# Loading a unit's imaginary gates ahead of its real ones, an earlier range check and a new hand-written order in a gated linear attention and soft-MoE kernel

## The chip, the cores and the metric

The kernel runs on 1 core of a Trainium2 chip. Its time is in device microseconds (us). Three runs of the kernel before gave 259.94, 262.14 and 263.29 us, so the median is 262.14 us; a separate execution was profiled.

## The reference

Inputs are q, k, v, a_re, a_im (each 4 x 8 x 768 x 48, float32) and the weights phi, w1, w2 of a soft mixture of experts. First a gated linear attention with complex gates, one step per token:

```python
mag = sqrt(a_re**2 + a_im**2); scale = minimum(mag, 0.999) / (mag + 1e-6)
ar, ai = a_re * scale, a_im * scale
for t in range(S):
    new_re = ar[t] * S_re - ai[t] * S_im
    new_im = ar[t] * S_im + ai[t] * S_re
    S_re, S_im = new_re + outer(k[t], v[t]), new_im
    y[t] = q[t] @ S_re
```

The result, 3072 tokens of 384 channels, goes through the mixture: `logits = x @ phi`; a softmax over the tokens gives 32 slot inputs; each of 8 experts computes `relu(slot @ w1) @ w2` (384 to 1024 to 384) for its 4 slots; a softmax over the slots mixes them back.

## The kernel before, in words

The attention is done in blocks of 128 tokens in polar form. A *unit* holds blocks of up to four batches; there are seven units, 0 and 6 of half size, since batches 2 and 3 lag one unit behind. Of a unit u the steps are, by their names in the order:

- `la{u}` (`load_a`, lines 620 to 626) loads the real gates `ar` and, as its second step, the imaginary gates `ai`, three DMAs of 256 KB each (two of 192 KB in unit 6). Both live in a pool with one buffer per name, so a load must wait until the unit before has read its own. Unit 0 is loaded by `load_first` and counts as two gate groups, `g0` and `g1`, so that unit u is group `g{u+1}`.
- `g` (`gates`, line 683): Ln of `ar` on ACT (line 689), Exp (691), a product into `ai` (DVE 695), a square (ACT 702 or DVE 700), Ln (704), a DVE step (706), Exp (708), a last DVE step (710). `t` (line 715): arctan of `ai` on ACT.
- `p{u}.{j}` (`phase`, 747): prefix sums of `ai` on PE (`sums`, 745, led by a carry matmul on tile `tk`, 743), a rounding (ACT 757 or DVE 755), a DVE step (760). `e{u}.{j}` (`logs`, 784): the same sums of `ar`, then two Exps on ACT (805, 807). `w` (`wave`): an absolute value (DVE 776) and two sines. `k` (`carry`): small steps that end in a PE transpose (734) and a copy to `tk`.
- `h{u}.{j}` (`mults`, 816): three products of q and k with these factors, each on DVE (814) or POOL (812). `M{u}` (`mixed`, 828): four DMAs on SP's queue that copy pieces into the tile `hm`, two after the second product, two after the third.
- `c` (`score`, 862, PE 867, then masked on DVE 879, or on ACT 881 and POOL 882), `a` (`attend`, PE 917 and 923, the result copied to `yT`), `x`, `D`, `f` (transposes, state, tokens) per batch; `l`, `s`, `sh`, `me`, `si` of the mixture's softmax; `hd`, `tn`, `ex`, `ou`, `er`, `mi` its experts, and outputs (`mi`: PE 296, a copy, a store).
- `q`, `v` load q and k, and v; `w_x` loads 1 MB of w1 or w2, in four pieces of 256 KB for x below 12. `T` and `L` preload the ACT table sets for sines and for logarithms. `zz` are pairs of matmuls with no use but activity on PE. `gd` (`ranges`, 1083) is a range check in six steps; its fifth is a PE matmul (1101).

All of this is sequenced by the string `ORDER` (line 306): each word runs a task's next step, and a star sends an operation that ACT or DVE could do (or DVE or POOL) to the other engine. `_InOrder` pins every engine, SP's DMA queue too, to this order. A DMA of a task named `la`, `q`, `v` or `w_` also waits for the last PE instruction traced before it, and a DMA on SP waits until it and those ahead of it under way come to at most 1.3 MB:

```python
for s, name in reversed(self.sent):
    n += s
    if n > UNDER_WAY:
        self.after(ins, name)
        break
```

PSUM serves most results through four buffers named `tr`.

Of the kernel before, what the change touches and what calls it, by code (L numbers as in the profile page):

```python
# [303 lines left out]


ORDER = """
    L0 g0 g0 g0 q1.1 g0* g1 g1 g1 g0 g1 g1 g0 g1 g0 g1 g0 g1 T0 t0 e0.2 e0.0 e0.1 e0.0 e0.1 t1 e0.2 L1 e0.0 e0.2 k0 la1 p0.1 e0.2
    e0.0 e0.1 p0.2 p0.0 p0.0 h0.0* p0.2* g2 g2 p0.1* p0.2 w0.2 p0.0 h0.2 la1 w_1 e0.1 T1 w0.2 w0.2 p0.1 w0.0 k0 q1.0 w_2 w0.0 w0.0
    zz10 g2* g2* h0.2 k0 h0.2 zz5 h0.1 zz13 zz6 h0.0 h0.1 h0.0 k0* M0 t2 p1.2 L2 g2 p1.2 g2 g2 M0 p1.2 v1 zz9 h0.1 p1.1 g2 w1.2
    p1.0 p1.1 p1.0 zz0 p1.1 T2 w1.2 q1.2 c0.0 e1.2 e1.2 w1.2 e1.1 L3 e1.2 p1.0 e1.2 c0.0* e1.0 la2 e1.1 e1.1 x0.0 w1.0 h1.2 e1.1  # L310
    h1.1 e1.0* e1.0 e1.0 la2 a0.0 h1.2 h1.0 x0.1 M1 a0.0 c0.1 x0.0* h1.2* q2.0 x0.0 x0.1 g3 g3 x0.1* T3 w1.0 w1.0 f0.0 c0.1* M1
    w_4 zz14 g3* a0.1 zz3 f0.0 zz12 w_0 q2.2 a0.1* zz1 zz4 k1 g3 h1.0 k1 D0.1 t3 k1* f0.1 D0.0 h1.1 h1.0 p2.2 h1.1 L4 g3 f0.1
    D0.0* D0.1 c0.2 p2.1 g3 q2.1 p2.2 c0.2 p2.0 g3 p2.2 p2.1* c0.3 w2.2 g3 a0.2 T4 w2.2 w2.2 c0.3 p2.0* e2.2 p2.1 a0.2* e2.2 e2.1
    p2.0 e2.1 e2.0 w2.0 L5 e2.2 e2.2 la3 e2.0 a0.3 e2.1 h2.2 x0.2 e2.1 h2.2 e2.0 x0.2 e2.0 la3 x0.2 c1.0 h2.1 k2 f0.2 D0.2 a0.3
    c1.0* D0.2 f0.3 f0.3 f0.2* x0.3 l0 x0.3* k2 c1.1 l0 h2.2* M2 g4 g4 l0 x0.3* h2.0 T5 w2.0 a1.0 g4* w2.0 D0.3 h2.1* k2 a1.0 l0*
    g4 c1.1* x1.0 D0.3 x1.0* h2.0 h2.0 M2 h2.1* x1.0 f1.0 a1.1 D1.0 f1.0* t4 v2 D1.0 a1.1 x1.1 x1.1* p3.2 p3.2* p3.2 x1.1 l0 q3.0
    w3.2 q3.2 p3.0 L6 g4 D1.1 s0 p3.0 g4 c1.2 c1.2 v3 q3.1 p3.1 g4 p3.0 c1.3 T6 w3.2 a1.2 p3.1* w3.2 g4 D1.1 p3.1 e3.2 e3.2 L7
    e3.2 s0 e3.0 c1.3* e3.1 e3.2 la4 a1.2 e3.1* w3.0 e3.0 la4 x1.3 h3.2 e3.0 a1.3 x1.3* e3.0 x1.3* e3.1 e3.1 h3.2 f1.1 h3.0 a1.3
    x2.0 f1.1* k3 x2.0 x1.2 x2.0 x1.2* c2.0 x1.2* g5 g5 T7 w3.0 w3.0 c2.0* D1.2 k3 D1.2 h3.2* h3.1 g5* f1.2 c2.1 k3 s0 a2.0 l1
    f1.2 M3 D2.0 a2.0* f1.3 l1 s0* c2.1* s0 M3 g5 t5 D1.3 w_3 h3.0* a2.1 s0 D1.3 h3.1* f1.3 D2.0 L8 g5 h3.0 f2.0 l1 f2.0* a2.1 l1*  # L320
    x2.1 p4.2 g5 q4.0 q4.2 p4.0 x2.1 g5 h3.1 l1 q4.1 x2.1 s1 p4.2 g5 p4.0 p4.1 c2.2 p4.2 e4.0 p4.0 c2.2 e4.0* e4.0 p4.1* e4.1 e4.2
    e4.0 p4.1 e4.1 e4.1 w4.2 s1 e4.2 la5 e4.1 e4.2 c2.3 e4.2 h4.2* w4.0 x2.2 c2.3* T8 w4.2 x2.2* x2.2* D2.1 a2.2 w4.0 D2.1 h4.0
    h4.1 a2.2 w4.2 la5 x2.3 x2.3 h4.2 w4.0 a2.3 x2.3* a2.3 x3.1 k4 x3.1* D2.2 h4.0* D2.2 x3.1* L9 g6 g6 M4 c3.0 l2 f2.2 f2.3 s1
    l2* c3.0* h4.2 M4 g6* f2.2* h4.1 a3.0 s1* f2.3* k4 l2 a3.0 l2 k4* x3.0 x3.0* c3.1 g6 x3.0 c3.1* h4.0* D2.3 D2.3 D3.0 l2 q5.2
    h4.1 s1 g6 a3.1 T9 t6 s1 g6 D3.0 v4 L10 g6 c3.2 c3.2* g6 p5.0 p5.1 a3.1 D3.1 p5.0 p5.1 q5.1 c3.3 p5.1 q5.0 s2 v5 p5.0 D3.1
    w5.0 s2 e5.2 c3.3 e5.2* x3.2 e5.1 e5.1 e5.2 e5.2 p5.2 x3.2 e5.0 h5.2 e5.1 p5.2* e5.1 e5.0 e5.0 a3.2 h5.1* x3.2 la6 e5.0 la6
    p5.2 T10 w5.0 f2.1 a3.2* x3.3 a3.3 w5.2 c4.0 w5.2 h5.0 f2.1 w5.2 x3.3 x3.3 w5.0 h5.2 a3.3* L11 g7 k5 g7 D3.2 x4.1 s2 s2* D3.2
    h5.2* c4.0* x4.1 x4.1* h5.1 l3 M5 l3* M5 a4.0 c4.1 x4.0 g7* f3.3 a4.0 x4.0 q6.2 h5.0 l3 x4.0 c4.1* D3.3 l3* a4.1 g7* g7 v6 w_5
    f3.3 k5 D3.3 f3.0 a4.1 k5* f3.0* h5.1 f3.1 f3.2 D4.0 h5.0 D4.1 f3.1* g7 c4.2 D4.0 q6.1 T11 t7 f3.2 p6.1 L12 g7 p6.1 c4.2* w_6
    p6.2 p6.0 p6.0 D4.1 g7 p6.0 p6.1 c4.3 e6.2 p6.2 e6.1 q6.0 p6.2 c4.3 e6.1 e6.2 e6.0 w6.2 e6.2 e6.0 e6.2 l3 T12 w6.2 we w_8 w6.2  # L330
    a4.2 h6.2 a4.2* L13 e6.0 w6.0 s3 e6.1 s2 s2 h6.2 h6.2 e6.0 w_7 M6 e6.1 a4.3 c5.0 M6 a4.3 c5.0* f4.2 x4.2 f4.2 T13 w6.0 x4.2*
    s3 w_9 l4 w6.0 h6.1 h6.1 h6.0* h6.0 a5.0 l4* c5.1 x4.2 l4 w_10 h6.0 s3 h6.1* a5.0 l4* s3 x4.3 D4.2 c5.1 x4.3 f4.0 c5.2 D4.2 l4
    f4.0* L14 s4 x4.3 s4 wf w_11 a5.1 a5.1 c5.2 zz8 s4 D4.3 D4.3 s3 s4* w_14 c5.3 a5.2 w_13 w_15 a5.2 f4.3 f4.3* s3 f5.0 f4.1 f5.1
    f5.1* w_16 f4.1* c5.3* a5.3 f5.0 a5.3 s4 l5 zz2 l5* s4 l5 w_17 l5* l5 me s5 f5.3 me sh f5.3* me w_12 me f5.2 s5 me s5 me me
    f5.2* s5 me s5 s5 zz11 sh ze si si zz15 sh hd sh er4 hd w_22 hd er2 hd hd hd w_21 hd gd er0 er4 hd hd w_18 hd tn0 er3 er4 tn0
    er3 er2 tn0* tn0 er1 er3 er2 ex0 hd w_19 gd ex0 ex1 er4 w_20 hd ex0 tn1 er1 tn1 tn1* er3 er0 ex0 tn1* er5 er0 er1 ex1 ex0 ex1
    ex0 ex1 er2 ex0 w_23 ex1 ex0 ou0 er1 ex1 ex1 er0 ou0 mi0.0 mi0.1 mi0.3 mi0.0* er5 mi0.4 ex2 er5 mi0.1* mi0.3* ex1 mi0.0 ou1
    mi0.4 er5 mi0.1 mi0.3 mi0.4 ex2 ex2 ou1 mi0.5 mi1.2 mi0.2 mi1.4 ex2 mi0.5 mi0.5 mi1.2* mi1.2 mi1.1 ex2 mi1.3 mi1.4* mi0.2
# [873 lines left out]
```

## Time and profile before

| | us |
|---|---|
| median of three runs | 262.14 |
| lowest, highest | 259.94, 263.29 |
| profiled execution | 262.23 |
| its span, first to last instruction | 260.7 |
| PE, DVE, ACT, POOL busy | 223.1, 189.5, 187.3, 62.3 |

The span leaves out 1.5 us around the first and the last instruction. An engine's busy time is not its bound: a wait counts only where it moves the chain of work to the end. In the views, a number in brackets is the idle time of the engine ahead of an instruction, with what ended it; `PEclk` is the granted TensorE clock as a share of 2.4 GHz.

### The profile page before, as it was taken

What the parts mean: (1) busy time and instruction counts of PE and PEld (TensorE: products, weight loads), DVE (VectorE), ACT (ScalarE), POOL (GpSimd) and SP (SyncE); (2) the same over time, 40 slices, a digit from 0 to 9 for tenths busy, and PEclk for the clock granted to TensorE, in tenths of its full rate; (3) what the DMA queues carried; (4) which work ended last, traced back from release to release, by engine and by line L of the source; (5) the groups of instructions that cost most, each with busy time, mean ns of one, the idle gap of its engine ahead of it and who ended that gap; (6) DMA issues with size and microseconds to landing.
All of it is one profiled execution on the core that took longest, in us unless ns stands there. A gap on an engine that the chain in (4) does not pass through costs nothing.

```text
span 260.7 us, 10985 instructions
## 1 busy us (share of the span) xinstructions
PE 223.1 (86%) x4828; PEld 177.1 (68%) x4828; DVE 189.5 (73%) x342; ACT 187.3 (72%) x296; POOL 62.3 (24%) x81
## 2 busy tenths in 40 slices
...
GB/s 168 277 265 259 285 158 247 256 250 190 275 127 157 283 173 282 42 270 185 198 109 64 166 263 146 162 125 231 252 254 240 240 291 425 424 400 343 370 363 137
DMA packets 28630, 60.96 MB, mean 234 GB/s; under 512 B 3232, under 2 KB 7584, under 8 KB 27040
## 3 DMA queue, kind: packets, MB, share of 16 engines
...
HBM read 49.17 MB, written 4.72 MB: 207 GB/s over the span
## 4 chain that ended last, share of the span: by engine, by line
PE 67%; DMA 12%; DVE 9%; ACT 5%; issue 3%; SPq 1%; DVEq 0%
PE qd L867 12%; PE qd L917 7%; PE qd L923 7%; PE lp L745 6%; PE up L745 5%; PE tp L852 4%; PE hp L230 4%; PE op L260 4%; DMA wx<-in_w_dram 4%; PE db L896 3%; DMA hm<-qe 3%; DMA ar<-in_aa_dram 3%; PE xp L931 2%; PE lg L115 2%; DVE scT L879 2%
## 5 line engine op out<-in xcount | busy, mean ns | idle before, releaser
L745 PE MATMUL lp<-cst,ar 128*128 128x128 f32 x144 | 20.9, 290 | 9.5 <-DVE ar L710 9.5
L879 DVE TENSOR_TENSOR scT<-qd,cst 128x1024 f32<-128x1024 f32 x16 | 19.5, 1221 | 11.9 <-ACT yT L106 7.4
L745 PEld LDWEIGHTS lp<-cst,ar 128*128 128x128 f32 x144 | 20.0, 203 | 10.5 <-DVE ar L710 10.0
L917 PE MATMUL qd<-scT,vt 128*48 128x128 f32 x352 | 23.8, 277 | 2.0 <-DVE scT L879 1.7
L745 PEld LDWEIGHTS up<-cst,ai 128*128 128x128 f32 x144 | 21.2, 213 | 4.4 <-ACT ai L715 1.7
L745 PE MATMUL up<-cst,ai 128*128 128x128 f32 x144 | 21.9, 297 | 2.6 <-ACT ai L715 1.4
L867 PE MATMUL qd<-e 32*128 32x128 f32 x384 | 23.0, 294 | 0.2 <-DVE scT L879 0.2
L106 ACT COPY yT<-qd 128x512 f32<-128x512 f32 x18 | 10.6, 592 | 16.9 <-PE qd L923 9.7
L917 PEld LDWEIGHTS qd<-scT,vt 128*48 128x48 f32 x352 | 18.2, 122 | 6.4 <-DVE scT L879 2.7
L867 PE MATMUL qd<-q 32*128 32x128 f32 x416 | 21.5, 274 | 0.0
L596 ACT ACT_TABLE_LOAD x15 | 19.2, 1283 | 1.3 <-PEq L1195 1.0
L867 PEld LDWEIGHTS qd<-e 32*128 32x128 f32 x384 | 16.3, 185 | 4.6 <-issue 1.9
L882 POOL TENSOR_SCALAR_AFFINE_SELECT scT<-scT 128x1024 f32<-128x1024 f32 x8 | 8.8, 1102 | 43.3 <-ACT scT L881 43.3
L867 PE MATMUL qd<-hm 32*128 32x128 f32 x352 | 18.3, 270 | 0.0
L599 ACT ACT_TABLE_LOAD x14 | 18.0, 1283 | 0.2
L867 PEld LDWEIGHTS qd<-q 32*128 32x128 f32 x416 | 17.2, 187 | 0.8 <-ACT d L106 0.6
L896 PE MATMUL db<-vt,kt 128*32 128x48 f32 x960 | 14.3, 208 | 3.4 <-issue 1.9
L896 PEld LDWEIGHTS db<-vt,kt 128*32 128x32 f32 x960 | 11.9, 110 | 6.6 <-issue 3.6
L762 POOL COPY cr<-fc 128x4 f32<-128x4 f32 x15 | 3.7, 250 | 51.0 <-DVE fc L760 50.8
L814 DVE TENSOR_TENSOR q<-q,fc 128x1024 f32<-128x1024 f32 (+1 forms) x13 | 14.6, 1140 | 0.2
L867 PEld LDWEIGHTS qd<-hm 32*128 32x128 f32 x352 | 14.6, 187 | 0.0
L812 POOL TENSOR_TENSOR qe<-qe,fc 128x512 f32<-128x512 f32 x8 | 11.9, 1506 | 9.7 <-DMA ar<-in_aa_dram 5.1
...
## 6 DMA issues: line engine op xcount, KB each, us to landing
...
```

Of the source, the lines that this page charges most:

```text
L106: self.nc.scalar.copy(out=out, in_=in_)
L230: self.nc.tensor.matmul(out=hp[x][32 * g : 32 * g + 32, :], lhsT=zs[hi][:, c, g, :], rhs=w1_chunk(12 * hi + 4 * c + g)[:, x * 512 : (x + 1 ...
L596: ACT.preload_act_table_set(LNEXP)
L599: ACT.preload_act_table_set(TRIG)
L745: PE.matmul(out=out[:, b], lhsT=gate[:, b, P * j : P * j + P], rhs=tri, start=not u, stop=not u or b == b1 - 1)
L812: POOL.tensor_tensor(out=out[:, w], in0=in0[:, w], in1=in1[:, w], op=ALU.mult)
L814: DVE.tensor_tensor(out=out, in0=in0, in1=in1, op=ALU.mult)
L867: PE.matmul(out=qd[:, i, P * g : P * g + P], lhsT=feat(u, g, c, 1, b)[r], rhs=feat(u, g, c, 0, b)[r], start=c == 0, stop=c == 2,)
L879: DVE.tensor_tensor(out=t, in0=sc, in1=mask.unsqueeze(1).unsqueeze(1).broadcast_to([P, 4, 2, P]), op=ALU.mult)
L896: PE.matmul(out=db[o, 3 * g + c], lhsT=kt[u, b][:, g, c, o], rhs=vt[u][:, b - _span(u)[0], 4 * g + i], start=True, stop=True)
L917: PE.matmul(out=o(g, i), lhsT=vt[u][:, b - _span(u)[0], 4 * g + i], rhs=scT[u, b][:, i, g], start=True, stop=not s)
L923: PE.matmul(out=o(g, i), lhsT=st[s - 1, b][r, 3 * g + c], rhs=feat(u, g, c, 0, b)[r], start=False, stop=c == 2)
```

## The change

`load_a` keeps its order (`ar`, then `ai`) in unit 1. From unit 2 on its first step takes the buffer of `ai` and loads it, and its second step does so for `ar`; each buffer is now asked for at the step that loads it.

```diff
     def load_a(u):
-        ar[u] = io.tile([P, UB, HD], F32, name="ar")
-        ai[u] = io.tile([P, UB, HD], F32, name="ai")
         b0, b1 = _span(u)
-        load(ar[u][:, b0:b1], aa[u, 0][:, b0:b1])
-        yield "la1"
-        load(ai[u][:, b0:b1], aa[u, 1][:, b0:b1])
+        parts = [(ar, "ar", 0), (ai, "ai", 1)]
+        if u == 1:
+            for held, name, _ in parts:
+                held[u] = io.tile([P, UB, HD], F32, name=name)
+        for held, name, k in parts if u == 1 else parts[::-1]:
+            if k != (u > 1):
+                yield "la1"
+            if u > 1:
+                held[u] = io.tile([P, UB, HD], F32, name=name)
+            load(held[u][:, b0:b1], aa[u, k][:, b0:b1])
```

`ORDER` is new throughout. It has the same words but two (`T13` and `L14` are gone, two of 29 table preloads); 91 steps change their engine by a star. Its beginning, up to the third unit, and its end, from the mixture's `ou2` on:

```diff
-    L0 g0 g0 g0 q1.1 g0* g1 g1 g1 g0 g1 g1 g0 g1 g0 g1 g0 g1 T0 t0 e0.2 e0.0 e0.1 e0.0 e0.1 t1 e0.2 L1 e0.0 e0.2 k0 la1 p0.1 e0.2
-    e0.0 e0.1 p0.2 p0.0 p0.0 h0.0* p0.2* g2 g2 p0.1* p0.2 w0.2 p0.0 h0.2 la1 w_1 e0.1 T1 w0.2 w0.2 p0.1 w0.0 k0 q1.0 w_2 w0.0 w0.0
-    zz10 g2* g2* h0.2 k0 h0.2 zz5 h0.1 zz13 zz6 h0.0 h0.1 h0.0 k0* M0 t2 p1.2 L2 g2 p1.2 g2 g2 M0 p1.2 v1 zz9 h0.1 p1.1 g2 w1.2
-    p1.0 p1.1 p1.0 zz0 p1.1 T2 w1.2 q1.2 c0.0 e1.2 e1.2 w1.2 e1.1 L3 e1.2 p1.0 e1.2 c0.0* e1.0 la2 e1.1 e1.1 x0.0 w1.0 h1.2 e1.1
-    h1.1 e1.0* e1.0 e1.0 la2 a0.0 h1.2 h1.0 x0.1 M1 a0.0 c0.1 x0.0* h1.2* q2.0 x0.0 x0.1 g3 g3 x0.1* T3 w1.0 w1.0 f0.0 c0.1* M1
-    w_4 zz14 g3* a0.1 zz3 f0.0 zz12 w_0 q2.2 a0.1* zz1 zz4 k1 g3 h1.0 k1 D0.1 t3 k1* f0.1 D0.0 h1.1 h1.0 p2.2 h1.1 L4 g3 f0.1
+    L0 g0 g0 g1 g0 g0* g1 g1 g0 g1 g1 g0 g1 g0 g1 T0 t1 g0 t0 g1 e0.2 k0 e0.0 e0.1 la1 e0.2 L1 e0.2 e0.0 e0.2 p0.2 p0.1 p0.2* e0.0
+    e0.0 h0.0 p0.2 p0.0 la1 e0.1 w_1 e0.1 e0.1 g2 p0.0* g2 w0.2 T1 w0.2 p0.1* p0.1 q1.0 p0.0 k0 h0.1 w0.0 k0 h0.2 g2* w0.0 g2* zz4
+    zz13 zz14 w0.0 q1.1 w0.2 h0.2 k0 zz1 h0.2 M0 t2 M0 w_2 h0.0 q1.2 L2 g2 h0.1 h0.0 p1.2 h0.1 g2 p1.1 p1.0 p1.2 g2 la2 c0.0 p1.2
+    p1.0 p1.1* w1.2 T2 w1.2 w1.2 g2 p1.1 zz9 e1.2 p1.0 e1.1 e1.0 e1.2 L3 e1.2 c0.0* w1.0 e1.1 e1.2 h1.2 la2 e1.1 h1.2 e1.0* e1.1
+    h1.1 a0.0 zz10 M1 x0.0 a0.0 e1.0 e1.0 x0.1 x0.0 h1.0 x0.0 g3 v1 w_0 c0.1 zz5 zz0 h1.2* M1 x0.1* x0.1* w_4 q2.1 q2.0 g3 c0.1*
+    T3 w1.0 q2.2 w1.0 a0.1 g3* g3 f0.0 zz12 a0.1* k1 zz3 zz6 f0.0 h1.0 h1.1 k1 h1.0 k1* D0.1 D0.0 f0.1 t3 L4 g3 h1.1 p2.2 D0.0
...
-    mi1.5 mi0.2 mi1.1* mi1.3* mi1.5* mi1.1 mi1.4 ex2 ex2 ex2 mi1.3 mi1.0 mi1.5 ou2 ou2 mi1.0* bh mi2.2 mi1.0 mi2.1 mi2.4 mi2.3
-    mi2.2* mi2.2 mi2.4* mi2.5 mi2.4 mi2.3 mi2.1* zz7 gd mi2.3 mi2.5* gd mi2.1 mi2.5 gd mi2.0 gd mi2.0* mi2.0
+    ex2 mi1.3 mi1.1* mi1.2* ex2 mi1.5* mi1.3* mi1.0 mi1.4 ex2 zz2 mi1.2 ou2 ou2 bh mi2.3 mi2.5 mi2.3 mi2.1 mi2.5* mi2.1 mi2.2
+    mi0.2 mi1.1 mi1.5 mi1.3 zz7 mi2.0 mi2.3 mi2.2* mi2.5 mi2.0 mi2.0 mi2.1 mi2.2 mi2.4 mi2.4 mi2.4
```

Elsewhere the range check's six steps stand ahead of `ou0`, the first of them before the last batches' attention; `w_3`, which came after `M3`, now comes after `la3` and ahead of `M2`; `v3` comes after `M3` where it came before `la4`; `la4`'s and `la6`'s first steps (now `ai`) come behind their units' last `p` instead of their last `e` or later.

## Rows read from the trace of the kernel before

**Rows 1.** Busy time by stretch (start:end, length, then busy us and count by engine).
```profile
9.50:24.00 14.50, 7.77 (x34) 5.30 (x34) 9.09 (x28) 12.10 (x22) 1.45 (x2) 1.00 0.78 259
24.00:31.00 7.00, 5.64 (x23) 4.78 (x24) 6.36 (x9) 5.63 (x5) 0.44 (x1) 0.52 0.84 269
42.00:54.00 12.00, 6.79 (x141) 4.42 (x141) 9.68 (x14) 10.71 (x11) 3.27 (x6) 1.00 0.84 245
60.00:214.00 154.00, 148.67 (x3786) 125.34 (x3782) 119.04 (x185) 122.62 (x195) 53.16 (x63) 1.00 0.63 196
219.80:250.00 30.20, 29.81 (x525) 18.50 (x524) 17.44 (x51) 10.04 (x20) 0.00 (x0) 1.00 0.97 386
```
**Rows 2.** Timeline of ACT at 43 us.
```profile
43.17 1.48 ACT L689 ACTIVATE ar<-ar 128x1536 f32<-128x1536 f32 x1 [2.57 <-issue]
```
**Rows 3.** Line 689, 36 to 48 us, and tile ar, 36 to 46: unit 2's loads.
```profile
L689 ACTq EVENT_SEMAPHORE  x1: 3084/3084/3084, 39.7 to 39.7; - x1
...
DMA to landing us min/median/max: 2.5/2.9/4.7
```
**Rows 4.** Tile ar, 62 to 69 us: the same for unit 3.
```profile
DMA to landing us min/median/max: 2.4/2.8/3.2
```
**Rows 5.** Timeline of SP's DMA queue, 36 to 75 us.
```profile
37.21 1.28 SPq L618 DMA_DIRECT2D ar<-in_aa_dram  x3
38.60 2.21 SPq L618 DMA_DIRECT2D ai<-in_aa_dram  x3
42.87 2.13 SPq L839 DMA_DIRECT2D hm<-qe  x2
48.62 8.00 SPq L618 DMA_DIRECT2D wx<-in_w_dram  x8
68.15 5.05 SPq L839 DMA_DIRECT2D hm<-qe  x4
```
**Rows 6.** Timeline of DVE, 16 to 24 us.
```profile
16.84 0.68 DVE L814 TENSOR_TENSOR qe<-qe 128x512 f32<-128x512 f32 x1
17.96 0.42 DVE L776 TENSOR_SCALAR fc<-fc 128x512 int32<-128x512 int32 x1
20.03 1.96 DVE L695 TENSOR_TENSOR ai<-ai,gt 128x384 f32<-128x384 f32 x4 [0.92 <-ACT gt L691]
```
**Rows 7.** Timeline of DVE, 38 to 42 us: the products of unit 1.
```profile
39.75 1.22 DVE L814 TENSOR_TENSOR qe<-qe,fc 128x1024 f32<-128x1024 f32 x1
```
**Rows 8.** Chain of waits in order of time: a copy into hm, and score c1.2.
```profile
47.47 3.98 DMA hm<-qe
...
84.44 1.55 PE qd L867 x48
```
**Rows 9.** Timeline of PE, 49 to 56 us.
```profile
52.67 0.39 PE L743 MATMUL up<-sf,tk 128*128 128x512 bf16 x1 [2.02 <-ACT tk L106]
54.43 0.40 PE L867 MATMUL qd<-hm 32*128 32x128 f32 x8
```
**Rows 10.** Groups of instructions of the whole run.
```profile
L695 DVE TENSOR_TENSOR ai<-ai,gt 128x384 f32<-128x384 f32 x22 | 10.8, 550 | 3.0 <-ACT gt L691 3.0
...
L596 ACT ACT_TABLE_LOAD x15 | 19.2, 1283 | 1.3 <-PEq L1195 1.0
```
**Rows 11.** Waits of PE, 60 to 214 us.
```profile
PE db L896 <- issue: 1.9, 1, 1.9
```
**Rows 12.** Timeline of all engines, 241 to 255 us.
```profile
241.95 1.33 SPq L303 DMA_DIRECT2D out_dram<-vt  x3
...
253.57 0.19 PE L1101 MATMUL gp<-cst,good 128*1 128x1 f32 x2 [1.40 <-DVE good L1098]
```
**Rows 13.** Stretches of the end: last two numbers are DMA share and GB/s.
```profile
242.00:244.00 2.00, 2.00 (x63) 1.76 (x65) 2.00 (x4) 1.06 (x2) 0.00 (x0) 1.00 0.97 394
254.00:256.00 2.00, 0.19 (x1) 0.00 (x0) 0.12 (x1) 0.59 (x1) 0.00 (x0) 1.00 0.96 353
256.00:258.00 2.00, 0.00 (x0) 0.00 (x0) 0.00 (x0) 0.00 (x0) 0.00 (x0) 0.52 0.33 108
```

More of the change, by code (lines that the diff above doesn't have):

```diff
@@ L315 @@
[L315 to L338, printed above, removed]
@@ new lines @@
+    D0.1 p2.2 g3 c0.2 p2.1 c0.2 p2.0 g3 c0.3 p2.2 la3 p2.0 p2.1* w2.2 g3 p2.1 f0.1* a0.2 e2.2 p2.0 c0.3* e2.1 T4 w2.2 w2.2 e2.0
+    la3 e2.2 L5 e2.2 e2.2 a0.2* e2.1 c1.0 w2.0 e2.1 e2.0 h2.2 e2.1 x0.2 e2.0 e2.0 a0.3 x0.2 x0.2 a0.3 h2.1 w_3 h2.2 f0.2 f0.2* k2
+    c1.0* M2 D0.2 D0.2* l0 h2.0 x0.3 f0.3 l0 f0.3 x0.3* g4 a1.0 x0.3* g4 T5 w2.0 a1.0* w2.0 h2.2* D0.3 c1.1 l0 D0.3* l0* M2 g4*
+    x1.0 k2 h2.0* f1.0 c1.1* x1.0* v2 q3.2 g4 a1.1 x1.0* k2 h2.1 x1.1 t4 f1.0* h2.1 p3.2 x1.1* h2.0* x1.1* p3.0 p3.1 a1.1 p3.2* L6
```

24 lines of the change are left out of this document (22 added, 2 removed).

## The prediction

> **What bounds the kernel now.** I read four views in this order. First the busy time by stretch, cut where PE changes its manner: the reader is to compare PE's busy time with the length of each stretch. From 60 to 214 us PE is busy 148.67 of 154.00 us and from 219.80 to 250 us 29.81 of 30.20, so there PE is the bound; its holes lie at the start, 6.73 us (14.50 - 7.77) from 9.5 to 24 us and 5.21 us (12.00 - 6.79) from 42 to 54 us [rows 1]. Second the waits of PE in the long middle: of its 5.3 us of holes the longest, 1.9, is "issue", in which no other engine is to blame [rows 11]. An order can win little there. Third the timelines of ACT, DVE and SP around the hole at 42 to 54 us. Fourth the end, where the reader is to look at the DMA columns: from 242 to 256 us they are 0.97 busy in the first stretch and 0.96 in the last, at 394 and 353 GB/s, and 0.33 after that [rows 13]. The last 15 us are shared by PE and the stores.
>
> Gains can therefore come from three places: the two early holes, and the end.
>
> **The change part by part.** The base is the profiled execution's 262.23 us (1.5 us of it outside the span); it lies 0.09 us above the median of 262.14, which I take off at the end.
>
> *ai ahead of ar.* In unit 2 ACT stood idle 2.57 us until 43.17 us ahead of Ln [rows 2], and its queue's semaphore wait of 3084 ns from 39.7 us names the DMA of ar: the three pieces took 2.5, 2.9 and 4.7 us to land [rows 3]. They were issued from 37.21 us and ai's right behind them, at 38.60 [rows 5]. In unit 3 the third piece took 3.2 us, with ai issued behind it too [rows 4]. With ai gone ahead (its last reader on PE, the sums of `p`, comes before those of `e`) ar should land like that: 4.7 - 3.2 = 1.5 us sooner. The bounds are 0 and the whole idle time of 2.57. In units 1 and 3 to 6 I cost the edit at nothing: the first consumer of ai is the product on line 695, and all its idle time, 3.0 us, is put down to ACT, none to a load [rows 10]; the cover is the two ACT passes ahead of it, and without them ai would cost its landing time. An early ai also stands in SP's queue and holds what is behind it until PE has passed the last sum of ai; in units 3 to 6 that is only ar and the copies of M, which wait for later work anyway.
>
> *The new order around unit 1.* Between the carry k0 and the product of g2, DVE gets three operations ahead: h0.1's first product and h0.2's, 0.68 each, and an absolute value, 0.42, together 1.78 us; at that place DVE was idle 0.92 [rows 6]. (What comes to DVE before k0, a product of 0.68 from POOL and a rounding of about 0.4 from ACT, is what went out.) So g2, its arctan, unit 1's sums and with them the last e of unit 1 come 1.78 - 0.92 = 0.86, say 0.9 us later, and so does the issue of ar. Bounds: 0, if ar of unit 1 lands sooner since q1.1 no longer goes ahead of it, and 1.8. What is left of the gain at the sums p2.2, which began at 52.67 after a wait of 2.02 us for ACT [rows 9], is 1.5 - 0.9 = 0.6.
>
> *SP's queue at the same place.* The next PE step but one, c0.2, reads hm from 54.43 us [rows 9]; the last copy into hm was issued at 47.47 and landed at 51.45 (47.47 + 3.98) [rows 8], which leaves 2.98 us. In the new order v1 (three pieces) and w_0 (four) go between M1's two halves, and q2.0 (two) goes behind: five pieces more. Held to 1.3 MB under way, pieces went at 8.00 / 8 = 1.00 us each [rows 5], which makes 5.0 us. Against it M1's first half can leave when its second product is done, at 40.97 (39.75 + 1.22) [rows 7], where it left at 42.87 behind ai [rows 5]: 1.9 us. So hm lands 5.0 - 1.9 - 2.98 = 0.1 us after its old reading time, and the 0.6 us won at p2.2 are lost at c0.2, on which ACT's copy of the scores and, behind it in ACT's order, the second half of g3 wait. I take **0** for the start as a whole. Its ends: -5.2, if all holes from 42 to 54 us close [rows 1], and +2.9: the 0.9 of DVE, and 2.0 if M1's first half leaves no earlier (5.0 - 2.98).
>
> *Other moved steps.* The `zz` pairs stay as many, but none now stands between the sums of unit 1. PE ran at 0.52 of full clock (that is mostly the 1.2 GHz level) from 24 to 31 us, after it had been busy 7.77 of the 14.50 us before [rows 1]. Its idle time ahead of unit 1's sums is about the same, so I take 0, with 0.9 either way (the extra time of one unit sum in that stretch). w_3 goes to about 70 us instead of 108 and puts four pieces, 4 us by the same rate [rows 5], ahead of M2's copies; these landed by 77.2 us (68.15 + 5.05 [rows 5] and 4.0) and are first read by c1.2 at 84.44 [rows 8], 7.2 us later, which hides it; without that cover it costs up to 4. v3 goes behind M3, well ahead of its first use.
>
> *Engines in the middle.* By row durations the new stars take about 4.6 us from ACT and give 5.0 to DVE, and the two table preloads that go, 1283 ns each [rows 10], take 2.6 us from ACT. No step of PE is added. DVE is busy 119.04 and ACT 122.62 of 154 us from 60 to 214 [rows 1], so neither is full and the swap lies beside PE: 0. Were DVE's share full at some place, it would cost up to 2 us; the holes of PE not named "issue" could give as much. Bounds -2 and +2.
>
> *The range check.* At the end PE waited 1.40 us for the check's DVE steps before its matmul of 253.57, and the last output's matmul stood behind it [rows 12]. All six steps now come before `ou0`, beside hidden and expert matmuls, where DVE is busy 17.44 of 30.20 us [rows 1]. So the last store can leave up to 1.4 us earlier. But the stores wait for bandwidth too: in the seven stretches of 2 us from 242 to 256 the DMA share is 0.91 to 1.04, and what is missing to 1 comes to 0.5 us [rows 13]; by that a full DMA would end only 0.5 us earlier. Against it stands that 18 stores of 0.262 MB, 4.72 MB, at the 394 GB/s of the first stretch take 12.0 us, and from the first issue at 241.95 [rows 12, 13] that is 253.9, where traffic ended near 256.7 (256 + 0.33 x 2): the rest is w_23 and the way of the first bytes. I take the middle of 0.5 and 1.4: **-1.0**, with bounds -1.4 and 0.
>
> The sum is 0 + 0 - 1.0: 262.23 - 1.0 = 261.2, and 0.1 off for the median: **261.1 us**.
>
> **The rivals.**
>
> *The hole closes.* If ar is all that holds the start, PE gets 5.2 us back and the check 1.4: 262.1 - 6.6 = 255.5. For it speaks that PE, DVE and ACT wait there in turn behind one late Ln; against it that ACT is busy 10.71 of those 12 us [rows 1], so it has little more than a microsecond to give.
>
> *ai was not in the way.* The third piece may be late by the bytes of ar itself, the DMA engines taking what SP issued in its order. Then the 1.5 us are not won, the 0.9 of DVE is lost, and the check gives 1.0: 262.1 + 0.9 - 1.0 = 262.0. For it speaks that ar's pieces were issued first, against it that unit 3's third piece was 1.5 us faster [rows 3, 4].
>
> The Trainium skill has a rule that speaks for this rival: in DMA: Bandwidth & Descriptors, section Queues, rings and completion order, each DMA engine is said to take descriptors of one ring in order, SP owning one row of rings, so a later load would not hold up an earlier one's start. By that rule the term of 1.5 would be 0; unit 2's 4.7 against unit 3's 3.2 us leaves it open, since both have ai behind ar.
>
> *Slower.* SP's queue holds hm. It decides if M1's first half doesn't leave before 42.9: then hm lands 2.0 us too late for c0.2, on top of DVE's 0.9, and the loads of q and k for unit 2 behind it slip as well. All PE work after c0.2 follows, and PE, full from 60 us on, can't make it up: +2.9. If the stores then give nothing back, since their bandwidth is the bound, the time is 262.1 + 2.9 = 265.0. For it speaks the rate of 1.00 us a piece, against it that ai's three pieces now leave ahead of ar's and are out of the way by then.
>
> *The middle loses.* A wait on one of the four tr buffers or on DVE costs 2 us: 263.1.
>
> **How the numbers follow.** Chances: the forecast 0.42 (its own range 259.5 to 262.5), the hole closes 0.13, ai not in the way 0.15, slower by SP's queue 0.20, the middle loses 0.10. The range takes in the slower rival and most of the way to the closed hole: 257.0 to 265.0 us; outside are about 0.1 below and 0.1 above. Two per cent, about what a measurement of this kernel can tell from no change, is 5.2 us. Below 256.9 lies most of the closed hole, 0.09; above 267.4 only a queue that slips further than worked out, 0.06; within stay 0.85.
>
> **What would show it right or wrong.** Right: ACT's idle time ahead of unit 2's Ln falls from 2.57 to near 1; PE waits at c0.2 for the DMA into hm; no PE wait for the check at the end, and the last store issued about 1 us earlier against the first. Wrong on the start: PE's hole from 42 to 54 us shrinks by 3 us or more, or hm comes over 1 us later than PE wants it. Wrong on the middle: PE's busy time between 60 us and the merge falls short of its length by more than 7.3 us or less than 3.3. The forecast falls if the median is under 259.5 or over 262.5.

## The result, and the profile after

The changed kernel took 263.78 us (median of 20, 260.40 to 268.15) against 261.42 for the kernel before on the same chips: ratio 1.0083, 95% interval 1.0054 to 1.0111, about 2.2 us. Here and below a ratio leaves out executions more than 1.5% above the fastest of the same kernel, so where the executions scatter it can lie under the quotient of the medians. A second measurement, in the experiments, gave 1.0031 (0.9982 to 1.0080), which by itself does not exclude no change. So it is slower, probably by some 1 to 2 us, where I had forecast a gain of 1.0 (262.1 to 261.1). The profiled execution, 262.22 us, lies 1.6 under its median; its span is 260.7 us, by chance that of the profile before.

Busy time of the changed kernel by the same stretches as [rows 1], with the merge (214 to 219.8 us) besides; the columns are PE, weight loads, DVE, ACT, POOL, granted clock, DMA share and GB/s:

```profile
9.50:24.00 14.50, 9.49 (x33) 6.33 (x33) 10.73 (x30) 11.82 (x19) 0.00 (x0) 0.88 0.60 197
24.00:31.00 7.00, 5.46 (x31) 4.86 (x35) 6.35 (x12) 5.24 (x5) 0.00 (x0) 0.76 0.85 263
42.00:54.00 12.00, 8.77 (x144) 5.60 (x140) 10.87 (x14) 10.36 (x10) 3.64 (x6) 0.86 0.87 257
60.00:214.00 154.00, 148.79 (x3803) 126.31 (x3803) 125.63 (x200) 119.11 (x191) 60.36 (x67) 1.00 0.65 198
214.00:219.80 5.80, 4.53 (x30) 1.75 (x26) 3.97 (x13) 0.41 (x2) 0.00 (x0) 0.76 1.01 425
219.80:250.00 30.20, 29.82 (x518) 17.89 (x510) 18.77 (x54) 9.41 (x17) 0.00 (x0) 0.99 0.93 375
```

PE's shortfall in the middle is 5.2 us (154.00 - 148.79), before 5.3. The busier PE from 42 to 54 us is no gain: the clock is at 0.86 there, and about as many matmuls (144 against 141) take longer. ACT's timeline around units 2 and 3, to be held against [rows 2]:

```profile
43.56 1.48 ACT L694 ACTIVATE ar<-ar 128x1536 f32<-128x1536 f32 x1 [2.88 <-DMA ar<-in_aa_dram]
...
71.52 1.48 ACT L694 ACTIVATE ar<-ar 128x1536 f32<-128x1536 f32 x1 [2.17 <-DMA ar<-in_aa_dram]
```

Unit 2's Ln waits as long as before, 2.88 us against 2.57, and unit 3's now waits 2.17. In the kernel before it did not wait (no bracket):

```profile
68.40 1.49 ACT L689 ACTIVATE ar<-ar 128x1536 f32<-128x1536 f32 x1
```

Unit 3's wait reaches PE. In ACT's order Ln, Exp, a table load and two sines stand ahead of a copy into the tile st, for which a transpose of the carry on PE waits 1.90 us (first ACT, then PE, in the changed kernel):

```profile
77.75 0.38 ACT L106 COPY st<-db 128x288 f32<-128x288 f32 x1
```

```profile
78.17 0.22 PE L739 MATMUL ctp<-idb,ct 128*128 128x128 bf16 x1 [1.90 <-ACT st L106]
```

Tile ar from 36 to 46 us, for [rows 3], and SP's queue, for [rows 5]:

```profile
DMA to landing us min/median/max: 3.6/4.0/4.1
```

```profile
35.25 2.13 SPq L618 DMA_DIRECT2D ai<-in_aa_dram  x3
37.76 2.44 SPq L618 DMA_DIRECT2D ar<-in_aa_dram  x3
40.59 1.69 SPq L844 DMA_DIRECT2D hm<-qe  x2
42.51 2.06 SPq L618 DMA_DIRECT2D vt<-in_vv_dram  x3
45.73 2.36 SPq L618 DMA_DIRECT2D wx<-in_w_dram  x4
50.32 1.11 SPq L844 DMA_DIRECT2D hm<-qe  x2
```

ar's three pieces took 1.28 us to issue before and take 2.44 now, right behind ai's, and each lands after 3.6 to 4.1 us instead of 2.5 to 4.7. The second half of hm leaves 3.9 us later than in the kernel before, where it was this row:

```profile
46.42 1.52 SPq L839 DMA_DIRECT2D hm<-qe  x2
```

PE's timeline where it reads hm, for [rows 9]:

```profile
52.93 1.16 PE L750 MATMUL up<-cst,ai 128*128 128x128 f32 x8 [0.47 <-ACT ai L720]
...
54.57 0.40 PE L872 MATMUL qd<-hm 32*128 32x128 f32 x8
```

No wait stands at the read of hm. The end, for [rows 12, 13], by stretches, then the first and the last store:

```profile
242.00:244.00 2.00, 2.00 (x50) 1.69 (x51) 1.04 (x2) 0.37 (x2) 0.00 (x0) 1.00 0.98 380
254.00:256.00 2.00, 0.00 (x0) 0.00 (x0) 0.29 (x1) 0.00 (x0) 0.00 (x0) 1.00 1.04 380
256.00:258.00 2.00, 0.00 (x0) 0.00 (x0) 0.00 (x0) 0.00 (x0) 0.00 (x0) 0.99 0.68 229
```

```profile
241.32 0.35 SPq L303 DMA_DIRECT2D out_dram<-we  x1
...
254.32 0.33 SPq L303 DMA_DIRECT2D out_dram<-wf  x1
```

PE no longer waits for the range check, but the bytes of the stores end later: 0.68 of the DMA share from 256 to 258 us, where it was 0.33. The last store leaves 13.0 us after the first (254.32 - 241.32), before 12.9 (from 241.95 to 254.84): it is no earlier against the first.

### The profile page after: what moved, and what is told of

Its sections match the earlier page's. It is cut to its first block, busy times and chain, and to the rows that moved or that the text cites. A ratio compares the mean times of both kernels' runs of the same rounds, so it can differ in the third digit from the quotient of the medians.

```text
span 260.7 us, 10973 instructions
## 1 busy us (share of the span) xinstructions
PE 225.9 (87%) x4828; PEld 177.9 (68%) x4828; DVE 199.0 (76%) x354; ACT 179.1 (69%) x281; POOL 67.7 (26%) x82
## 4 chain that ended last, share of the span: by engine, by line
## 5 line engine op out<-in xcount | busy, mean ns | idle before, releaser
L750 PEld LDWEIGHTS lp<-cst,ar 128*128 128x128 f32 x144 | 19.9, 203 | 12.2 <-DVE ar L715 11.7
L884 DVE TENSOR_TENSOR scT<-qd,cst 128x1024 f32<-128x1024 f32 x17 | 20.7, 1218 | 9.4 <-ACT yT L106 8.1
L872 PE MATMUL qd<-e 32*128 32x128 f32 x384 | 22.0, 294 | 0.6 <-ACT scT L886 0.5
L106 ACT COPY yT<-qd 128x512 f32<-128x512 f32 x16 | 9.4, 588 | 14.6 <-PE qd L928 11.3
L767 POOL COPY cr<-fc 128x4 f32<-128x4 f32 x15 | 2.8, 188 | 61.3 <-DVE fc L765 61.3
L872 PEld LDWEIGHTS qd<-e 32*128 32x128 f32 x384 | 15.6, 185 | 3.9 <-issue 0.9
L817 POOL TENSOR_TENSOR q<-q,fc 128x512 f32<-128x512 f32 (+1 forms) x12 | 15.3, 1300 | 7.3 <-PE qd L928 4.8
L817 POOL TENSOR_TENSOR qe<-qe,fc 128x512 f32<-128x512 f32 x8 | 12.9, 1633 | 11.5 <-DVE qe L819 9.1
L700 DVE TENSOR_TENSOR ai<-ai,gt 128x384 f32<-128x384 f32 x22 | 14.1, 699 | 2.0 <-ACT gt L696 2.0
L694 ACT ACTIVATE ar<-ar 128x1536 f32<-128x1536 f32 (+2 forms) x8 | 9.3, 1164 | 8.8 <-DMA ar<-in_aa_dram 8.8
L819 DVE TENSOR_TENSOR q<-e,q 128x1024 f32<-128x1024 f32 (+1 forms) x12 | 14.8, 1240 | 0.3 <-ACT e L812 0.3
```

Source lines behind the costliest of these rows:

```text
L106: self.nc.scalar.copy(out=out, in_=in_)
L694: ACT.activation(out=r, in_=r, func=AF.Ln, bias=TINY)
L700: (DVE if moe.other else POOL).tensor_tensor(out=i[:, b], in0=i[:, b], in1=t[:, b], op=ALU.mult)
L750: PE.matmul(out=out[:, b], lhsT=gate[:, b, P * j : P * j + P], rhs=tri, start=not u, stop=not u or b == b1 - 1)
L817: POOL.tensor_tensor(out=out[:, w], in0=in0[:, w], in1=in1[:, w], op=ALU.mult)
L819: DVE.tensor_tensor(out=out, in0=in0, in1=in1, op=ALU.mult)
```

## The experiments

Every ratio is to the kernel before, run on the same chip in turn, with its 95% interval.

### First: the change cut into load order, start, middle and end

The other half of the edit in `load_a` (each buffer asked for at its own step), with ar still first, leaves the program the same, instruction by instruction and wait by wait. So the first run measures the order of the two loads alone: five pairs of loads on SP change places and nothing else.

```diff
 ORDER: as before
-        load(ar[u][:, b0:b1], aa[u, 0][:, b0:b1])
-        yield "la1"
-        load(ai[u][:, b0:b1], aa[u, 1][:, b0:b1])
+ load_a as changed: ai, yield, ar, for u > 1
```

Expected: 

> The order of before, with only load_a changed (from unit 2 on ai ahead of ar, each buffer asked for when its own piece is loaded). My step 1 gives ai ahead of ar 0 to -1.5 us by itself, and by the rival 'ai was not in the way' 0. So 1.000 of before (0.995 to 1.002). If putting ai first is itself what made the changed kernel slower (ar late for the Ln of unit 2), this run shows the whole +0.8%, about +2.2 us.

Measured: 272.0 us, **1.0389** (1.0323 to 1.0455), 10 us slower. ACT's timeline of this kernel shows where, at the Ln of units 2, 3 and 4 (the profiled execution, 274.20 us, lies 2.2 above the median):

```profile
46.03 1.48 ACT L694 ACTIVATE ar<-ar 128x1536 f32<-128x1536 f32 x1 [5.17 <-DMA ar<-in_aa_dram]
...
76.45 1.49 ACT L694 ACTIVATE ar<-ar 128x1536 f32<-128x1536 f32 x1 [3.73 <-DMA ar<-in_aa_dram]
...
111.21 1.48 ACT L694 ACTIVATE ar<-ar 128x1536 f32<-128x1536 f32 x1 [4.92 <-DMA ar<-in_aa_dram]
```

These three Ln began at 43.17, 68.40 and 98.97 us before: the lag grows to 2.9, 8.1 and 12.2 us, unit by unit. All of ACT's waits for ar come to 16.6 us. In the kernel before they come to 6.4: 3.8 that the view puts down to the DMA, and unit 2's 2.57, which it calls "issue". First this kernel, then the kernel before:

```profile
ACT ar L694 <- DMA ar<-in_aa_dram: 16.6, 7, 5.2
```

```profile
ACT ar L689 <- DMA ar<-in_aa_dram: 3.8, 4, 1.2
...
ACT ar L689 <- issue: 2.6, 1, 2.6
```

The cause is in SP's queue and in PE's timeline (first SP, then PE, then SP's waits from 30 to 40 us):

```profile
37.55 1.28 SPq L618 DMA_DIRECT2D ai<-in_aa_dram  x3
38.94 2.32 SPq L618 DMA_DIRECT2D ar<-in_aa_dram  x3
```

```profile
36.43 1.05 PE L750 MATMUL lp<-cst,ar 128*128 128x128 f32 x8
```

```profile
SPq L618 <- PE lp L750: 3.2, 1, 3.2
```

The reader is to compare 37.55 with 36.43 + 1.05 = 37.48: ai does not leave when its last sums of `p` are done, but when the last sum of `e` is, behind which its step stands in the old order. So it takes the place in time that ar had (37.21), and ar goes 1.7 us later and more slowly.

The three other kernels have the changed `load_a` too and one part each of the new order. The cuts lie where both orders have done the same steps but for one to three: at `L4` (52 us) and at the shares of the merge (216 us).

```diff
 e2_start_new:  new order up to L4, then the order of before
 e3_middle_new: before up to L4, new up to sh, then before
 e4_tail_new:   before up to sh, then new
```

Expected of the start: 

> The new order up to the Ln/Exp table load that follows unit 2's arctan (some 52 us), then the order of before; load_a as changed. Theory S (start): the new order leaves TensorE idle for 2.8 us at 43 us, with its warming matmuls behind the wait, and the granted clock falls there (0.57 from 46 to 50 us, 1.00 before): this run then has the whole loss, about +2.2 us (1.008), and a granted clock below 1 at 46 to 50 us. Theories M (middle) and T (tail): 1.000, within 0.3%.

Of the middle: 

> The order of before up to 52 us and from the shares of the merge on, the new order between (52 to about 216 us); load_a as changed. Theory M: the re-arranged middle costs what the changed kernel lost, +2.2 us (1.008), as my rival 'the middle loses' (+1 us) had it. Theories S and T: 1.000 or, by the profile of the changed kernel, whose expert matmuls begin 2.1 us earlier (217.70 against 219.79), down to 0.992.

Of the end: 

> The order of before up to the shares of the merge (about 216 us), then the new order, the range check ahead of the experts; load_a as changed. My step 6 gives -1.0 us (0.996; bounds -1.4 and 0). Theory T: the loads of the last stage and the stores stand in a worse order, and this stage alone loses what the changed kernel lost, +2.2 us (1.008). Theories S and M: 0.995 to 1.000.

Measured: 1.0198 (1.0103 to 1.0292), 1.0192 (1.0132 to 1.0253) and 1.0357 (1.0278 to 1.0437). None of the theories stood, since all had the order of the loads at nothing. Read against the 1.0389 of the first run, the new start takes back 1.9 points (0.0389 - 0.0198), the new middle 2.0 and the new end 0.3, which is within the intervals: taken in this sequence, the new order pays for ai going first.

### Second: what the new order does to the loads

```diff
 ORDER: as changed
-        for held, name, k in parts if u == 1 else parts[::-1]:
+        for held, name, k in parts:
-            if k != (u > 1):
+            if k:
```

Expected: 

> The changed kernel with one thing undone: ar is loaded ahead of ar's partner ai again, in the new order; each buffer is still asked for at its own step. Theory A (ai ahead of ar is the loss): in the changed kernel ACT waits 2.88, 2.17 and 0.58 us for ar ahead of the Ln of units 2, 3 and 4, together 5.6 us; two pieces fewer ahead of ar, at about 1 us each, take most of that away, so this kernel runs 2 to 5.6 us under the changed one, at 0.985 to 1.000 of before. Rival B (the new order needs ai first, since it asks for the buffers before ar's is free, and ar at the head of the queue then holds everything behind it): 1.008 of before or more. Rival C (the loss is the clock or the tail): 1.008, as the changed kernel.

Measured: 1.0203 (1.0114 to 1.0293), as rival B has it and outside theory A's range. That it is slower than the changed kernel is less certain: two kernels with ai first, on the same chip (the third set of experiments), gave 1.0112 and 1.0145, and the intervals overlap. ACT's waits for ar do not decide it either. They come to 5.8 us here and to 8.8 and 8.2 in two profiles of the changed kernel, but to 6.4 and 5.6 in those two kernels, which load as the changed one does. SP's waits over the whole run, first in this kernel, then in the changed one:

```profile
SPq L618 <- PE lp L750: 11.4, 5, 3.7
...
SPq L618 <- DVE ar L715: 6.8, 2, 3.4
```

```profile
SPq L618 <- PE lp L750: 6.3, 2, 3.7
...
SPq L618 <- DVE ar L715: 4.6, 2, 3.5
```

The new order asks for the first buffer behind the last `p`. If that is ar, SP stands until PE has read the former ar in `e`, and what is behind it in the queue stands too. In five profiles of the whole new order with ai first SP's wait for the sums of `e` is 5.9 to 8.5 us; with ar first it is 11.4 here and 13.1 in a later kernel.

```diff
 load_a: as changed; ORDER of before, but for u = 2..6
-... p.(u-1) ... e.(u-1) ... la(u) ... la(u)
+... p.(u-1) la(u) ... e.(u-1) ... la(u)
```

Expected: 

> The order of before with ai first, as in the experiment that was 3.9% slower, and one thing more: the step that loads ai stands right behind the last sum that reads the former ai, units 2 to 6 (in unit 2 nineteen words earlier, in unit 3 twenty-five), ar's step unmoved. Theory A1 (ai's three pieces stand between SP and ar: what counts is when ar is issued and how many bytes are under way just then): ai is out of the way by then, most of the 10 us go: 1.000 to 1.010. Theory A2 (an early ai only holds SP's queue until its buffer is free, and ar is late by the place of its own step, the second one): no gain, 1.03 to 1.04.

Measured: 1.0218 (1.0123 to 1.0313). Moving ai's step alone gives back 1.7 of the 3.9 points. Its SP queue at unit 2:

```profile
32.80 3.40 SPq L618 DMA_DIRECT2D ai<-in_aa_dram  x3
...
38.75 1.58 SPq L618 DMA_DIRECT2D ar<-in_aa_dram  x3
```

ai leaves 4.75 us sooner than in the first run (32.80 against 37.55). ar gains little, 38.75 against 38.94, because q1.2's two pieces now go between them. So neither theory's range held the result. Place and what else is queued both seem to count, and what is left of the 2.2% was not taken apart further.

### Third: the range check and the warming pairs

```diff
 n6: ORDER as changed, gd x6 where before has them
-... ze me me s5 ... si si gd sh ... hd hd gd er4 ...
+... hd gd ... zz7 gd mi2.0 mi2.3 gd mi2.2* mi2.5 gd mi2.0 gd mi2.0
```

Expected: 

> The changed kernel with the six steps of the range check back at the places that they have in the order of before, the last four at the end. By my step 6 (the check at the end costs 1.4 us of waiting, of which 1.0 reaches the end) this is 1.0 us slower than the changed kernel: 1.012 of before. If the stores' bandwidth is the bound at the end and the check lies beside it: equal to the changed kernel, 1.008. If the early check is what costs: 1.000.

Measured: 1.0112 (1.0037 to 1.0187). This cannot be told from the changed kernel, 1.008, nor from the 1.012 of my step 6, so it does not settle whether the early check gains 1.0 us. In the profile PE waits 0.9 us for the check again, and from the first store's issue to the end of the span it is 20.1 us, where both profiles of the changed kernel have 19.4.

```diff
-... zz5 zz0 h1.2* M1 ... a0.1 g3* g3 f0.0 zz12 a0.1* k1 zz3 zz6
+... zz5 zz0 zz12 zz3 zz6 h1.2* M1 ... a0.1 g3* g3 f0.0 a0.1* k1
```

Expected: 

> The changed kernel with three pairs of warming matmuls moved from behind unit 0's last but one output block to ahead of it, into the 2.76 us in which TensorE waits for the scores at 43 us. Rival C (the granted clock, 0.57 from 46 to 50 us in the changed kernel and 1.00 before, carries the loss): the clock stays at 1.00 there and the time falls to 1.000 to 1.004. Theory A: the clock may rise, the time stays at 1.006 to 1.010, since ACT and the late ar set the pace there.

Measured: 1.0145 (1.0079 to 1.0211). The stretch of 46 to 50 us in this kernel, for the clock:

```profile
46.00:50.00 4.00, 3.06 (x117) 2.35 (x113) 3.71 (x7) 3.99 (x4) 0.00 (x0) 1.00 0.73 235
```

The clock is up, 1.00 where it was 0.57 (and down to 0.87 and 0.80 from 50 to 60 us), and the time is not better: what it lacks at 46 to 50 us does not carry the loss. That fall comes in some executions of both kernels: the second profile of the changed kernel, with no edit, has 1.00 there, and the second one of the kernel before has 0.58.

```profile
46.00:50.00 4.00, 4.00 (x124) 2.89 (x119) 4.00 (x8) 3.99 (x7) 0.00 (x0) 1.00 0.73 224
```

```profile
46.00:50.00 4.00, 4.00 (x43) 1.64 (x43) 3.79 (x8) 3.99 (x4) 0.97 (x3) 0.58 0.84 268
```

### Fourth: the merge's clock, and ar first in part

In the profile of the changed kernel PE's first 34 hidden matmuls behind the merge take 5.39 us, partly at the 1.2 GHz level (granted clock 0.76 from 214 to 219.8 us):

```profile
217.70 5.39 PE L230 MATMUL hp<-wx,xs 128*32 128x512 f32 x34 [0.37 <-DVE xs L223]
```

Before, the same 34 took 4.06, at 2.4 GHz:

```profile
219.79 4.06 PE L230 MATMUL hp<-wx,xs 128*32 128x512 f32 x34
```

They took over 5 us in four of the five profiles with the new middle that there were then. Four kernels test that.

```diff
 a2: the changed kernel again
 m1: as changed
-... me s5 me s5 me zz15 me si si gd ... zz2 ... zz7
+... me s5 me s5 zz7 me zz15 me si si zz2 gd
 m2: m1, and ar first for u = 2..5
 k1: the kernel before
-... s5 s5 zz11 sh ze si si zz15 sh hd ... zz7 gd
+... s5 s5 sh ze si si sh hd ... zz7 zz15 zz11 gd
```

Expected of the changed kernel: 

> The changed kernel itself once more, as the measure for the three others on the same chip, and for a second profile of it. 1.006 to 1.012 of before. Theory K (in the changed kernel the granted clock falls in the merge, at 214 to 222 us, and the first 34 hidden matmuls of the experts run partly at the lower level): these take over 5 us in this profile, against 4.06 before. Theory Q (what is lost lies with the order of the loads of ar and ai alone): nothing is said on them.

Of the two pairs in the merge: 

> The changed kernel with two pairs of warming matmuls, which stood at the very end, moved into the merge: one ahead of the sum of the weights, one ahead of the first hidden matmul, where PE waits 0.44 and 0.37 us for DVE. Theory K: the clock stays at 1.00 in the merge, the first 34 hidden matmuls take 4.06 us instead of the 5.4 to 6.6 that four of five profiles of the new middle show (mean of the five 5.64, so 1.6 us), and the time falls by about 1 to 1.5 us under the changed kernel: 1.001 to 1.006 of before. Theory Q, or the last stage being set by its loads: the clock rises and the time stays with the changed kernel.

With ar first as well: 

> As the kernel with the two pairs in the merge, and ar ahead of ai again in units 2 to 5, not in the last unit, where in the new order q, k and v stand between the two loads. Theory A (ACT waits for ar because ai is ahead): the waits ahead of the Ln of units 2 and 3, 2.88 and 2.17 us in the changed kernel, shrink, and the time falls by another 1 us: 0.995 to 1.002 of before. Rival B (ar at the head of SP's queue, asked for before its buffer is free, holds what is behind it): slower than the kernel with the two pairs alone, 1.010 or more.

Of the kernel before without its pairs: 

> The kernel before with the two pairs of warming matmuls of the merge moved to the end, where TensorE waits 1.40 us for the range check. Theory K: the clock falls in the merge as in the changed kernel, the first 34 hidden matmuls take 5.4 to 6.6 us in place of 4.06, and the time rises by about 1 to 2 us: 1.004 to 1.008 of before. Without K: 4.06 us and 1.000.

Measured: 1.0031 (0.9982 to 1.0080), 1.0057 (1.0001 to 1.0113), 1.0101 (1.0045 to 1.0157) and 0.9976 (0.9934 to 1.0018). As a cause of the median, theory K fell twice: with the pairs the changed kernel is not faster, without them the kernel before is not slower. The profiles show both sides. The kernel before without its pairs, in the execution profiled (267.09 us, where its median is 261.98), then its clock from 222 to 226 us:

```profile
221.00 6.83 PE L230 MATMUL hp<-wx,xs 128*32 128x512 f32 x34 [0.37 <-DVE xs L223]
```

```profile
222.00:226.00 4.00, 4.00 (x24) 0.83 (x20) 3.36 (x19) 0.00 (x0) 0.00 (x0) 0.50 1.00 420
```

And the changed kernel with the pairs, the 34 matmuls and PE's waits behind them:

```profile
221.27 4.06 PE L230 MATMUL hp<-wx,xs 128*32 128x512 f32 x34
```

```profile
233.54 1.95 PE L260 MATMUL op<-q,scT 128*32 128x128 f32 x64 [1.29 <-DMA q<-in_w_dram]
...
246.22 1.03 PE L260 MATMUL op<-wx,scT 128*32 128x128 f32 x29 [1.04 <-DMA wx<-in_w_dram]
```

A fall of the clock costs up to 2.8 us (6.83 - 4.06) where it happens, and it doesn't happen in every execution: the changed kernel's own second profile had 4.06 us. In the profile with the pairs, where the clock stays up, PE runs into the weights instead: 1.29 + 1.04 us of waiting for DMA, with the DMA share at 1.00 and more from 226 to 246 us. But in the changed kernel's second profile, with the clock up as well, the wait for the weights is 0.3 us, so it isn't shown that the gain is given back there in every execution.

With ar first in units 2 to 5, ACT's waits for ar come to 6.6 us in place of 9.5 with the pairs alone, and the time is not better, 1.0101 beside 1.0057 with the intervals overlapping: the further 1 us of theory A is not there. None of the versions tried is faster than the kernel before beyond its interval.

### Fifth: each order with the loads made for it

```diff
 d1: new order up to L4, ai first in unit 2; rest as before
 d2: new order from L4 to sh, ai first in units 3..6; rest as before
 d3: new order from sh; rest as before, ar first throughout
 b2: the kernel before again
```

Expected of the start: 

> The new order up to 52 us with ai first in unit 2, whose loads stand there, then the order of before with ar first in units 3 to 6: each order with the order of loads that was made for it. Theory S2 (what the changed kernel loses, it loses in the start, where ACT still waits 2.88 us for ar, v1 and w_0 go ahead of the masks' copies and the clock is down at 46 to 50 us): 1.004 to 1.010 of before. Theories M2 (middle) and T2 (end): 0.997 to 1.002.

Of the middle: 

> The order of before up to 52 us with ar first in unit 2, the new order up to the shares of the merge with ai first in units 3 to 6, the end of before. Theory M2 (ACT waits 2.17 us for ar ahead of the Ln of unit 3, and the hidden matmuls behind the merge fall to the lower clock more often): 1.004 to 1.010 of before. Theories S2 and T2: 0.997 to 1.002.

Of the end: 

> The order of before with ar first everywhere up to the shares of the merge, then the new order, with the range check ahead of the experts. By my step 6: 0.996 of before (-1.0 us; bounds -1.4 and 0). Theory T2 (the new end lets the stores out later against the outputs: 19.4 us from first store to the end of the span in two profiles of the changed kernel, 18.75 before): 1.002 to 1.004. If the stores' bandwidth sets it: 1.000.

Of the control: 

> The kernel before itself, as measure on the same chip and for a second profile: 1.000 (0.996 to 1.004). For the theory on the clock in the merge (K): the first 34 hidden matmuls take 4.06 us here as in the first profile; over 5 us would show that the fall comes by chance in both orders.

Measured: 1.0032 (0.9983 to 1.0082), 1.0008 (0.9939 to 1.0076), 1.0024 (0.9982 to 1.0066), control 0.9986 (0.9943 to 1.0028). The three ratios add to +0.6%, as much as the two measurements of the whole, and none is clear of no change. But the first two kernels scatter, 259.81 to 264.94 and 258.54 to 269.45 us. The medians of all twelve, 263.57, 263.72 and 262.01 us, against 261.47 for the kernel before on that chip, are 0.8%, 0.9% and 0.2% above it. So a loss of 1 to 2 us in the start or in the middle is not excluded; only the end is close to nothing by both. The start's profile shows a lower clock than the control's, 0.50 against 0.76 from 24 to 31 us, though the first profile of the kernel before had 0.52 [rows 1]. In the changed start, PE's wait ahead of that stretch, then the stretch:

```profile
19.67 0.29 PE L739 MATMUL ctp<-idb,ct 128*128 128x128 bf16 x1 [3.52 <-DVE ct L736]
```

```profile
24.00:31.00 7.00, 5.04 (x20) 4.24 (x21) 6.35 (x10) 4.96 (x5) 0.00 (x0) 0.50 0.85 271
```

PE had stood idle 3.52 us ahead of that, where the order of before has a warming pair in between. But unit 2's second Ln (of 1 plus the squares, line 704 before and 709 after) begins at 52.8 to 54.4 us in five profiles with the new start and its loads (the changed kernel's two, m1, n6, d1), and at 53.2 to 54.4 in five with the old one: within that spread PE's clock in the start costs nothing that arrives at 54 us.

The middle has the wait that unit 3's late ar passes on to PE. By the profiles, the wait of unit 3's Ln for ar and PE's wait for the copy into st are, in us:

| kernel | Ln for ar | PE for st |
|---|---|---|
| changed, first and second profile | 2.17, 2.47 | 1.90, 1.77 |
| with the two pairs in the merge | 2.71 | 2.49 |
| with the late check | 1.11 | 0.89 |
| new middle with its loads | 0.79 | 0.57 |
| with the pairs at 43 us | 0.17 | none |
| new middle, ai first in units 2 to 6 | none | none |
| new order, ar first (two kernels) | none | none |

The second profile of the changed kernel, at the Ln and at PE:

```profile
70.63 1.49 ACT L694 ACTIVATE ar<-ar 128x1536 f32<-128x1536 f32 x1 [2.47 <-DMA ar<-in_aa_dram]
```

```profile
77.28 0.22 PE L739 MATMUL ctp<-idb,ct 128*128 128x128 bf16 x1 [1.77 <-ACT st L106]
```

PE's wait follows ar's in size. In the order of before a wait of 0.7 to 1.1 us for DVE stands at 82 to 83 us that the new order is without, so the new one costs about 1 us more where ar is late. It is of the size of the loss, but it varies from one execution to the next, and the kernels that load ar first are without it and no faster (1.0203 and 1.0101).

One rival is untested, the clock over the whole execution. Averaged over the span, the granted clock is 0.962 and 0.960 in the two sets of executions of the changed kernel, 0.964 with the new start alone, 0.970 with the new middle and 0.978 with the new end; in five sets of the kernel before it is 0.971 to 0.975. By an estimate from these figures, 0.012 less is about 6 us more of an execution at 1.2 GHz (0.012 / 0.5 x 261). No run raised that mean back (0.965 with the pairs in the merge, 0.963 with the pairs at 43 us), so whether it costs time or only follows from PE's waits is open.

## Why the prediction was wrong, point by point

*ai ahead of ar*: **this step failed**, and with its sign. I took 1.5 us off unit 2's landing, with bounds 0 and 2.57, and put units 3 to 6 at nothing since ai's consumer never waited. The consumer that matters is ar's. In the changed kernel unit 2's Ln waits 2.88 us for ar, where I had about 1, and unit 3's waits 2.17, where I had nothing, and of this 1.90 us reach PE in the middle, which I had called full. In the order of before the edit alone costs 10 us: ar's pieces leave 1.7 us later at unit 2, ACT waits for them 16.6 us in place of 6.4, and the lag adds up from unit to unit. In the new order this does not hold: there ar first (1.0203 and 1.0101) is no better than ai first. I had reasoned on when ai's buffer comes free, not on when SP gets to its step, and I compared landing times of ar with ai behind it in both cases, so that nothing in my rows spoke of ai ahead. The Trainium skill's rule that I weighed (DMA: Bandwidth & Descriptors, Queues, rings and completion order: on each DMA engine the descriptors of a ring are taken in order) fits this: with ai ahead, ar's pieces left SP 1.7 us later. I had used it only to doubt my gain, and not asked what it makes of an ai put ahead. It gives no price for that, and no run here separates the order in a ring from the order in which SP issues.

*The new order around unit 1*, *SP's queue*, *other moved steps*: I took 0 for the start as a whole, and by unit 2's second Ln 0 it is (about 54 us in both, above), but not by my terms. The new order moves ai's step forward, in unit 2 to 35.25 us ahead of the last sums of `e`, and that is part of how it wins back what the loads lose; I had read the move as harmless and given it no price. DVE's product began 0.5 us later in unit 1 (20.55 against [rows 6]), where I had 0.9. hm's second half left 3.9 us later, more than I worked out, and PE did not wait for it: the rival with hm fell.

*Engines in the middle*: 0 is not settled. PE's shortfall is 5.2 us against 5.3 in the first two profiles, but 7.7 in the second of the changed kernel (154.00 - 146.35, with 54 matmuls fewer on record), beyond the 7.3 that I had named as a sign of being wrong. DVE gained 6.6 us of work (125.63 - 119.04), where I had 5.0.

*The range check*: -1.0 is not borne out, and what the check gains is not settled. The new end alone came to 1.0024 (0.9982 to 1.0066), so a full 1.0 us (0.9962) lies outside; late against early in the new order (1.0112 and 1.0083) can't tell 1 us from 0. PE's wait is gone, the stores still end when their bytes are through. From the first store's issue to the end of the span are 18.8 and 19.5 us in the two profiles of the kernel before and 19.4 in both of the changed one. Over all profiles it is 18.8 to 21.2 us with the late check (ten profiles, mean 19.9) and 18.6 to 19.8 with the early one (eight, mean 19.4), which leaves room for half a microsecond.

I forecast -1.0 us and measured +0.8 to +2.2 (ratios 1.0031 and 1.0083 of 261.5). Of this miss up to 1.0 is the check. The rest, the loss of 1 to 2 us, is the remainder of terms that I had at zero: going from the kernel before, ai first costs 10 us and the order that goes with it wins about 8; going the other way round, the new order with ar first is 1.0203 and ai first takes that back in part. Where the remainder lies is **not settled**. PE's wait behind unit 3's late ar is one part that the profiles show, about 1 us net in those of the changed kernel; the clock at 46 to 50 us and in the merge does not carry it, the clock over the whole execution is untested, and what the check gains is open below 1 us.

The range, 257.0 to 265.0, held the median, and my own range for the forecast, 259.5 to 262.5, did not. That the wide range held it was luck, since it was made for hm and for the closed hole, and neither came. The rivals "the middle loses" (263.1), "slower" (265.0) and "ai was not in the way" (262.0) lay closer. The first comes nearest to the reason: PE does wait in the middle, but for an ACT copy behind a late ar, not for a tr buffer or DVE.
